# Seven-product second layer: the first product is copied by ScalarE into another product's PSUM bank, the products run in another order, and the sums of quarters come in fewer pieces

## Chip, cores and metric

The kernel runs on one core of one Trainium2 chip. The metric is the time of the program on the device, in microseconds (us), as the median of several runs. Beside the times there is one execution recorded by the hardware profiler; all durations of single instructions come from that one.

## What is computed

For 8 sequences of 576 tokens with 8 heads of width 64: attention over a sliding window of 128 keys with a bias that falls with the distance; then, for each token's 512 values, a normalisation, a layer of 512 to 2048 with a ReLU, a second layer of 2048 to 512, and the sum with the layer's input.

```python
scores = scale * q @ k.T - slope[head] * distance    # only 0 <= distance < 128, else -1e9
attn = softmax(scores)
x = concat_heads(attn @ v)                           # (8, 576, 512)
xn = (x - mean(x)) / sqrt(var(x) + 1e-6) * g_ln
out = x + maximum(xn @ w_ch1, 0.0) @ w_ch2           # (512 x 2048), (2048 x 512)
```

## The kernel before

**Blocks and groups.** The tokens are cut into 36 blocks of 128 (per pair of sequences 8 whole blocks and one, T, that holds the 64 last tokens of both). A block's attention gives a tile `x` of 128 tokens by 512. The two layers run on groups of blocks: groups 0 to 3 have two blocks each, groups 4 to 10 four. Group 10 has a form of its own for both layers (`mlp1_last`, `mlp2_last`). This text is about groups 4 to 9.

**First layer** (`mlp1`, matmuls in L866). Sixteen units, one for each 128 of the 2048 hidden values: four matmuls of 128x512 into one PSUM bank, then a ReLU to `ht_all`, by ScalarE (L882), or for units 6 and 13 by VectorE (L874).

**Second layer of groups 4 to 9** (`mlp2_seven`, matmuls in L1096). The 2x2 block product (512 tokens in a top and a low half, 2048 hidden values in two halves, 512 outputs in a left and a right half) is made with seven products in place of eight. Four of them take sums of quarters of the hidden values, made by VectorE in `sum_hidden` (L916): s1 = a21 + a22, s2 = s1 - a11, s3 = a11 - a21, s4 = a12 - s2. Each quarter is 128 x 8 x 256; a sum can be made in pieces of its 8 parts. A product is 16 matmuls of 128x256 into one PSUM bank (8 for each of the two blocks of a half, which lie side by side in the bank). It is cut into four units of four matmuls, so that the layer has units 0 to 27. Products add up in PSUM in three banks called x, t and y, and after each product VectorE adds the bank, scaled by the token's `rstd`, onto two output tiles `o` (`onto`, L1117, two instructions). The seven, in the order before:

| place | bank | product | then added onto |
|---|---|---|---|
| 1 | x (fresh) | a11 b11 | top left |
| 2 | t (fresh) | a12 b21 | top left |
| 3 | x | s2 t2 | top right |
| 4 | y (fresh) | s1 t1 | low right |
| 5 | x | s3 t3 | low right |
| 6 | y | s4 b22 | top right, then the top half is stored |
| 7 | x | a22 t4 | low left, then the low half is stored |

Because x goes on growing, product 3 may not start before `onto` has read what product 1 left in x, and product 5 not before `onto` has read what product 3 left.

**Order of the work.** The engines' orders are written out by hand: TensorE (PE) runs the units of the layers, and between them, at places listed in `TWICE` and `LEAD`, steps of the attention of later blocks. A block n has four steps: *go* (scores, and the exponential of one half of them, L509), *step* (values, L594, into PSUM; then on VectorE reciprocal L602, x L603, mean L631 and xc L635), *exps* (the exponential of the other half), and *rest* (VectorE multiplies the new probabilities by the mask, L531, one or two instructions; ScalarE squares xc, L679, for the variance; DMA transposes are issued). In groups 5 to 8 the first layer holds go, step, exps, rest of one block and go, step, exps of the next; the second layer holds *rest* and *go* behind unit 0, *step* and *exps* behind unit 5, *rest* behind 8, *go* behind 12, *step* and *exps* behind 19, *rest* behind 23. In group 9 only the first five of these nine are left. `weave_at` puts the pieces of sums of `SUMS_AT` behind a unit of the first layer, ahead of the attention steps of the same place; the dictionary `more` does the same with what it lists, for either layer (sums of first-layer weights for group 10, L916 too, and from unit 20 of group 9 on the sums of its inputs).

Each engine runs its instructions in the order in which they are written, and waits where a semaphore isn't there yet; what is written behind waits too.

Of the kernel before, what the change touches and what calls it, by code (L numbers as in the profile page):

```python
# [50 lines left out]
SUMS_AT = {  # L51
# [5 lines left out]
}  # L57


# [36 lines left out]
def kernel(  # L96
# [10 lines left out]
    nc = tc.nc  # L107
# [426 lines left out]
    def attends(p, blk):  # L534

        low, high, every = [0, 1], [2, 3], [0, 1, 2, 3]
        if blk == T:
            return [(p, T, [6, 7], m_ends, "probs", hps) for hps in (low, high)]
        if blk < 2:
            return [(p, blk, [blk], m_full[:, :, P:], "own", every)]  # L540
        return [(p, blk, [blk - 2, blk], m_full, "probs", hps) for hps in (low, high)]
# [5 lines left out]
    def tail_attend(p):  # L547
        return (p, T, [T], m_tail, "own", [0, 1, 2, 3])
# [169 lines left out]
    for g, size in enumerate(GROUPS):  # L718
        n = sum(GROUPS[:g])
# [67 lines left out]
    for n in range(8, ONE_GO):  # L787
        ahead = place[min(n + AHEAD, count - 1)]
        todo = []
# [23 lines left out]
    for n in range(ONE_GO, count):  # L813
        todo = []
        if n + 1 < count and order[n + 1][1] == T:
            todo.append(tail_attend(order[n][0]))
        if n + 2 < count:
            todo += attends(*order[n + 2])
        first_of, pairs = n == ONE_GO, (1, 0) if len(todo) > 1 else (0,)
        go = [(attend, *a, sc, first_of or sc == 1, sc == 0) for a, sc in zip(todo, pairs)]  # L820
        step = [(load_until, place[min(n + AHEAD, count - 1)]), (masks,) + order[n]]
        step += [(values_at_once, *order[n], 1), (centre,) + order[n]]
        rest = [(masks, *args[:2], 1) for args in todo] + [(square, n)]
        for tag, m in (("q", n + 5), ("k", n + 6)):
            if m < count and order[m][1] % 2 == 0:
                p, blk = order[m]
                (step if first_of else rest).append((turn_natural, tag, p, blk // 2))
        steps += [go, step, [(exps,)], rest]
    TWICE = [1, 4, 5, 7, 7, 11, 12], [0, 0, 5, 5, 8, 12, 19, 19, 23]
    LEAD = [([2, 2, 4, 4, 7, 7, 9, 9, 12, 13], TWICE[1])]  # L830
    LEAD += 4 * [TWICE] + [(TWICE[0], TWICE[1][:5]), ([], [])]
    done = 0

    def advance_to(n):
        nonlocal done
        while done < min(n, len(steps)):
            for f, *args in steps[done]:
                f(*args)
            done += 1
# [69 lines left out]
    half = NFB // 2  # L909
    left, right = slice(0, DM // 2), slice(DM // 2, DM)  # L910
    b11, b12 = w2[:, 0:half, left], w2[:, 0:half, right]
    b21, b22 = w2[:, half:NFB, left], w2[:, half:NFB, right]
    t1, t2, t3, t4 = (w2sums[:, i] for i in range(4))
# [148 lines left out]
    hsums = {}  # L1062
# [20 lines left out]
    def mlp2_seven(g):  # L1083


        ht = hidden[g]
        s = [hsums.pop((g, i)) for i in (1, 2, 3, 4)]
        a11, a12, a22 = ht[:, 0:half], ht[:, half:NFB], ht[:, half:NFB]

        def product(ps, lhs, off, rhs, first):  # L1090


            for pair in range(2):
                at = off + pair * P
                for fb in range(half):
                    nc.tensor.matmul(  # L1096
                        ps[:, pair, :],
                        lhs[:, fb, at : at + P],
                        rhs[:, fb, :],
                        start=(first and pair == 0 and fb == 0),  # L1100
                        stop=(fb == half - 1),
                        skip_group_check=True,
                    )
                    if fb % 4 == 3 and not (pair == 1 and fb == half - 1):
                        yield

        outs = {}

        def onto(ps, blocks, cols, fresh):

            for pair in range(2):
                at = 2 * blocks + pair
                p, blk = members[g][at]
                n = p * NSLOT + blk
                if at not in outs:
                    outs[at] = out_pool.tile([P, DM], FP32, tag="o", name="o")
                nc.vector.scalar_tensor_tensor(  # L1117
                    out=outs[at][:, cols],
                    in0=ps[:, pair],
                    scalar=rstd[:, n : n + 1],  # L1120
                    in1=(xs[p, blk] if fresh else outs[at])[:, cols],
                    op0=ALU.mult,
                    op1=ALU.add,
                )

        def leave(blocks, cols=slice(0, DM)):
            for pair in range(2):
                store(*members[g][2 * blocks + pair], outs[2 * blocks + pair], cols)

        def bank2():  # L1130
            t = ps_mm.tile([P, DM], FP32, tag="mm", name="ps_s")
            return t.rearrange("p (r d) -> p r d", r=2)

        top, low = 0, 1
        x = bank2()
        yield from product(x, a11, 0, b11, True)
        onto(x, top, left, True)
        yield
        t = bank2()
        yield from product(t, a12, 0, b21, True)  # L1140
        onto(t, top, left, False)
        yield
        yield from product(x, s[1], 0, t2, False)
        onto(x, top, right, True)
        yield
        y = bank2()
        yield from product(y, s[0], 0, t1, True)
        onto(y, low, right, True)
        yield
        yield from product(x, s[2], 0, t3, False)  # L1150
        onto(x, low, right, False)
        yield
        yield from product(y, s[3], 0, b22, False)
        onto(y, top, right, False)
        leave(top)
        yield
        yield from product(x, a22, 2 * P, t4, False)
        onto(x, low, left, True)
        leave(low)
        yield  # L1160
# [103 lines left out]
    def weave_at(units, *places, seven=None, sums=None, more={}):  # L1264


        advance_to(done + places.count(-1))
        for u, _ in enumerate(units):
            for f, *args in more.get(u, []):
                f(*args)  # L1270
            if seven is not None:
                if u == 1:
                    inv_std(sum(GROUPS[:seven]), len(members[seven]))
                for i, c in SUMS_AT.get(u, []):
                    sum_hidden(seven, i, c)
            if sums is not None and u % 4 == 1:
                sum_w2(sums + u // 4)
            advance_to(done + places.count(u))
# [13 lines left out]
    with tc.manual_schedule(engines={engine.PE}):  # L1292
        with tc.manual_schedule(engines={engine.Activation, engine.DVE, engine.SP, engine.Pool}):
            start()
            advance_to(first)
            weave_at(mlp1_pair((0, 12), (0, 8), (12, NFB), (8, NFB)), 1, 2, 3, 3, 7, 7, 9, 18, 24, 28)
            weave_at(mlp2(0, ((0, 8), (8, 12), (12, NFB))), 1, 4, 8, 10, 10, 12)
            weave_at(mlp2(1), 1, 3, 5, 7, 9, 13, 13)
            weave_at(mlp1(2), 0, 4, 7, 9, 14)
            weave_at(mlp2(2), 1, 5, 9, 13, 13, 15, 15)  # L1300

            weave_at(mlp1(3, (9, 10, 11)), 4, 7, 8, 10, 12, 15, sums=0)
            weave_at(mlp2(3), 0, 2, 3, 6, 9, 11, 12, sums=4)
            last = len(GROUPS) - 1
            for g in range(4, last):
                one, two = LEAD[g - 4]
                early, late = ({u: [(sum_w1, i)] for u, i in at.items()} for at in W1_SUMS_AT.get(g, ({}, {})))
                if g == last - 1:  # L1310
                    late[20] = [(sum_x, last, i) for i in (1, 2)]
                    late[24] = [(sum_x, last, i) for i in (3, 4)]
                    late[26] = [(inv_std, sum(GROUPS[:last]), len(members[last]))]
                weave_at(mlp1(g, (6, 13)), *one, seven=g, more=early)
                weave_at(mlp2_seven(g), *two, more=late)
            units = mlp2_last(last)
            scores_psum.close()
            ps_last = pool("ps_last", 1, space=PSUM)
            LAST_SUMS_AT = {
                u: [(sum_hidden, last, 3 + u % 2, (c, c + half // 2))]  # L1320
                for u, c in ((2, 0), (4, half // 2), (3, 0), (5, half // 2))
            }
            mlp1_last(last, lambda: next(units), ps_last)
            weave_at(units, more=LAST_SUMS_AT)
# [31 lines left out]
```

## Time and profile before

| | us |
|---|---|
| median of 3 runs | 309.24 (308.67 to 309.47) |
| the profiled execution | 309.44 |
| its span, first to last instruction | 307.7 |
| granted TensorE clock over the span | 0.994 |
| TensorE matmuls busy | 294.9 (96%) |
| VectorE busy | 240.7 (78%) |
| ScalarE busy | 180.1 (59%) |
| groups 4 to 9, both layers | about 94 to 279 us of the span |
| group 10 and the last stores | about 279 to 307.7 us |

A line of the timeline reads: start in us from the span's beginning, duration of the (merged) instructions in us, engine, line, operation, output <- inputs with shapes, xcount, and in brackets how long the engine had been idle before and what released it. DVE is VectorE, ACT is ScalarE, PEld TensorE's weight loads. A 128x256 matmul is recorded with 0.27 us, but the next one starts 0.109 us later: eight of them are in the records as 1.03 or 1.04 us and keep TensorE for 0.87. So the idle time that the profile gives for TensorE behind a matmul is about 0.16 us less than the time by which the next matmul was late, and in this text a delay of TensorE is counted from start to start.

### The profile page before, as it was taken

Reading aid. Unit: us, or ns where it says so; the run is one execution under the profiler, and the core shown is the slowest. Engines: PE = TensorE matmul, PEld = TensorE weight load, DVE = VectorE, ACT = ScalarE, POOL = GpSimd, SP = SyncE. Lnnn points to the kernel's source line nnn. Section 1 sums busy time; section 2 is a strip of 40 time slices with the busy share of each in tenths; the row PEclk is TensorE's granted clock in tenths of the full one; section 3 lists DMA queues with packets and bytes.
Section 4 is the critical chain, followed back from the end, with each engine's and each line's share of the span. In section 5 each row is a group of like instructions: output and inputs, shape, how many; then the busy total and the mean of one; then the engine's idle time right before and its main releaser. Section 6 shows DMA issues by size and latency. Waiting matters only on the chain.

```text
span 307.7 us, 9278 instructions
## 1 busy us (share of the span) xinstructions
PE 294.9 (96%) x3778; PEld 201.8 (66%) x3778; DVE 240.7 (78%) x646; ACT 180.1 (59%) x332; POOL 112.5 (37%) x153
## 2 busy tenths in 40 slices
PE   6799999999999999999999999999999999899994
PEld 2377745866855568656765686468656865688883
DVE  2578868779896698759876987598889878968993
ACT  4487776858967863477347734773577357405500
POOL 8933559783773480684017161760000000000000
PEclk9799999999999999999999999999999999999999
DMA  9999999999999999999979999999472053005014
GB/s 96 171 200 201 191 152 154 200 141 100 142 127 160 163 143 144 166 183 150 120 120 130 148 116 152 141 132 133 89 129 46 19 87 86 19 19 137 2 34 102
DMA packets 150074, 38.03 MB, mean 124 GB/s; under 512 B 140656, under 2 KB 145920, under 8 KB 150032
## 3 DMA queue, kind: packets, MB, share of 16 engines
q0 software_dynamic: 103792, 18.46, 86.9%
q1 hardware_dynamic: 45760, 18.60, 39.8%
q8 instruction: 29, 0.48, 0.7%
q10 hardware_dynamic: 480, 0.39, 0.5%
q14 instruction: 13, 0.11, 0.1%
HBM read 36.90 MB, written 9.44 MB: 151 GB/s over the span
## 4 chain that ended last, share of the span: by engine, by line
PE 75%; DVE 13%; DMA 5%; ACT 2%; issue 2%; POOL 1%; DVEq 0%; POOLq 0%
PE ps_m L866 28%; PE ps_s L1096 18%; PE ps_m L896 9%; PE ps_sc L498 5%; DVE s L916 5%; PE ps_q L1175 4%; PE ps_sc L594 4%; DMA xT<-xc 3%; PE ps_x L990 3%; DVE probs L531 2%; DVE x L603 2%; DMA first<-in_k_dram 2%; DVE o L1117 1%; DVE xc L635 1%; PE ps_tr L346 1%
## 5 line engine op out<-in xcount | busy, mean ns | idle before, releaser
L866 PE MATMUL ps_m<-xT,w1g 128*128 128x512 f16 (+1 forms) x512 | 104.0, 353 | 0.1
L882 ACT ACTIVATE ht_all<-ps_m 128x512 f16<-128x512 f32 (+1 forms) x143 | 71.3, 512 | 35.2 <-PE ps_m L866 32.7
L866 PEld LDWEIGHTS <-w1g 128*128 128x128 f16 x512 | 47.7, 98 | 41.4 <-issue 0.3
L509 ACT ACTIVATE probs<-ps_sc 128x1024 f16<-128x1024 f32 x56 | 55.6, 1021 | 8.9 <-PE ps_sc L498 8.7
L289 POOL DMA_DIRECT2D vx<-in_v_dram x40 | 34.1, 862 | 72.4 <-PE ps_sc L594 59.4
L1096 PE MATMUL ps_s<-w,s 128*128 128x256 f16 x384 | 44.9, 273 | 2.0 <-DVE o L1117 2.0
L1096 PEld LDWEIGHTS <-s 128*128 128x128 f16 x384 | 36.8, 98 | 7.4 <-issue 2.8
L679 ACT ACTIVATE junk<-xc 128x512 f16<-128x512 f16 x28 | 17.6, 629 | 40.3 <-DVE xc L635 40.3
L531 DVE TENSOR_TENSOR probs<-probs,m 128x1024 f16<-128x1024 f16 x56 | 36.2, 683 | 2.0 <-ACT probs L509 2.0
L1096 PE MATMUL ps_s<-w,ht_all 128*128 128x256 f16 x288 | 35.2, 273 | 0.0
L896 PE MATMUL ps_m<-w,ht_all 128*128 128x512 f16 x128 | 31.5, 380 | 0.0
L1096 PEld LDWEIGHTS <-ht_all 128*128 128x128 f16 x288 | 27.4, 98 | 4.6
L278 POOL DMA_DIRECT2D q<-in_q_dram x40 | 27.6, 708 | 4.1 <-PE ps_m L866 1.9
L916 DVE TENSOR_TENSOR s<-ht_all 128x1024 f16<-128x1024 f16 (+2 forms) x36 | 20.5, 568 | 7.9 <-ACT ht_all L882 7.0
L498 PEld LDWEIGHTS <-k 64*64 64x64 f16 x1088 | 16.1, 108 | 13.7 <-issue 12.5
L498 PE MATMUL ps_sc<-q,k 64*64 64x128 f16 (+1 forms) x1088 | 22.1, 215 | 1.0 <-issue 0.7
L603 DVE SCALAR_TENSOR_TENSOR x<-ps_sc,rec 128x512 f16<-128x512 f32 x32 | 22.1, 691 | 1.1
L1117 DVE SCALAR_TENSOR_TENSOR o<-ps_s,rstd,x 128x256 f32<-128x256 f32 x48 | 20.8, 475 | 2.2 <-PE ps_s L1096 2.2
L275 POOL DMA_DIRECT2D k<-in_k_dram x20 | 17.9, 911 | 6.8 <-DMA k<-k 5.6
L1117 DVE SCALAR_TENSOR_TENSOR o<-ps_s,rstd,o 128x256 f32<-128x256 f32 x36 | 15.7, 477 | 5.8 <-PE ps_s L1096 5.7
L602 DVE RECIPROCAL rec<-ps_sc 128x8 f32<-128x8 f32 x32 | 6.4, 201 | 16.8 <-PE ps_sc L594 16.7
L594 PEld LDWEIGHTS <-probs 128*128 128x128 f16 x384 | 15.9, 98 | 3.6
(117 smaller groups left out, 376.6 us busy)
## 6 DMA issues: line engine op xcount, KB each, us to landing
out_dram<-o SPq DMA_DIRECT2D x64, 128.0 KB, 3.4
vx<-in_v_dram POOLq DMA_DIRECT2D x32, 128.0 KB, 7.5
w<-in_moe_w_ch_dram POOLq DMA_DIRECT2D x8, 512.0 KB, 11.7
k<-in_k_dram POOLq DMA_DIRECT2D x30, 128.0 KB, 7.5
q<-in_q_dram POOLq DMA_DIRECT2D x48, 64.0 KB, 6.2
q<-in_q_dram POOLq DMA_DIRECT2D x10, 128.0 KB, 7.3
out_dram<-o SPq DMA_DIRECT2D x10, 64.0 KB, 1.9
k<-in_k_dram POOLq DMA_DIRECT2D x8, 64.0 KB, 7.2
```

The source lines that it names most:

```text
L289: nc.gpsimd.dma_start(out=vx[p0 : p0 + n, :, 0:D], in_=v[b, :, t0 : t0 + n, :].rearrange("h p d -> p h d"),)
L498: nc.tensor.matmul(in_halves(ps[cols, j, n, t, :])[:, r, queries], kt[rows, hp, cols], in_halves(qt[rows, b, hp])[:, r, queries], start=no ...
L509: nc.scalar.activation(out=dst.rearrange("p (n j) q -> p j n q", j=2), in_=ps.rearrange("p j n t q -> p j n (t q)"), func=AF.Exp, scale=in ...
L531: nc.vector.tensor_tensor(out=dst, in0=dst, in1=mask, op=ALU.mult)
L594: nc.tensor.matmul(ps[:, h, 0 : D + 1], pr[:, h, t, :], vext[(p * NSLOT + o) % NV][:, h, :], start=(n == 0), stop=(n == len(terms) - 1),)
L603: nc.vector.scalar_tensor_tensor(out=x.rearrange("p (h d) -> p h d", h=H), in0=ps[:, :, 0:D], scalar=1.0, in1=rec.unsqueeze(2).broadcast_t ...
L866: nc.tensor.matmul(ps[:, 0:cols], w[:, kb, fb * P : (fb + 1) * P], xT[:, kb, 0:cols], start=(kb == 0), stop=(kb == NKB - 1),)
L882: nc.scalar.activation(out=ht[:, fb, :], in_=ps[:, 0:cols], func=AF.Relu)
L896: nc.tensor.matmul(sums[at], ht[:, fb, at * P : (at + 1) * P], w2[:, fb, :], start=(fb == 0), stop=(fb == NFB - 1),)
L916: nc.vector.tensor_tensor(out=out, in0=a, in1=b, op=op)
L1096: nc.tensor.matmul(ps[:, pair, :], lhs[:, fb, at : at + P], rhs[:, fb, :], start=(first and pair == 0 and fb == 0), stop=(fb == half - 1), ...
L1117: nc.vector.scalar_tensor_tensor(out=outs[at][:, cols], in0=ps[:, pair], scalar=rstd[:, n : n + 1], in1=(xs[p, blk] if fresh else outs[at] ...
```

## The change

In `mlp2_seven` all three banks are taken at the start. After product 1 VectorE no longer adds x onto the output; ScalarE copies bank x into bank t (128x512, fp32), and the product a12 b21 is later accumulated in t on top of the copy, so that one `onto` adds both. The places are now: 1 x: a11 b11, copy to t; 2 y: s1 t1, onto low right; 3 x: s2 t2, onto top right; 4 t: a12 b21, onto top left; 5, 6 and 7 as before. So a group has six `onto` in place of seven.

The sums of quarters: before, s1, s2 and s4 came in three pieces each (parts 0 to 2 behind unit 11 of the first layer, 3 to 5 behind unit 14, 6 and 7 behind unit 15). Now s1 has the same three pieces, s2 two (parts 0 to 2 behind unit 11, 3 to 7 behind unit 15), and s4 is one instruction over all 8 parts, behind unit 4 of the second layer. s3 stays.

In the attention of blocks 12 to 35, the squaring of a block with n % 4 = 1 moves from its own *rest* to the *rest* of block n + 2. In group 9 the *rest* of block 34 moves from behind unit 0 of the second layer to behind unit 14 of the first, after the piece of s1 there.

```diff
 SUMS_AT = {
     5: [(3, (0, 4))],
     8: [(3, (4, 8))],
-    11: [(1, (0, 3)), (2, (0, 3)), (4, (0, 3))],
-    14: [(1, (3, 6)), (2, (3, 6)), (4, (3, 6))],
-    15: [(1, (6, 8)), (2, (6, 8)), (4, (6, 8))],
+    11: [(1, (0, 3)), (2, (0, 3))],
+    14: [(1, (3, 6))],
+    15: [(1, (6, 8)), (2, (3, 8))],
 }
...
-        rest = [(masks, *args[:2], 1) for args in todo] + [(square, n)]
+        rest = [(masks, *args[:2], 1) for args in todo]
+        rest += [(square, m) for m in {1: (), 3: (n - 2, n)}.get(n % 4, (n,))]
...
-    LEAD += 4 * [TWICE] + [(TWICE[0], TWICE[1][:5]), ([], [])]
+    LEAD += 4 * [TWICE] + [(TWICE[0] + [14], TWICE[1][1:5]), ([], [])]
...
-        s = [hsums.pop((g, i)) for i in (1, 2, 3, 4)]
+        s = [hsums[g, i] for i in (1, 2, 3)]
...
         top, low = 0, 1
-        x = bank2()
+        x, t, y = bank2(), bank2(), bank2()
         yield from product(x, a11, 0, b11, True)
-        onto(x, top, left, True)
+        nc.scalar.copy(out=t, in_=x)
         yield
-        t = bank2()
-        yield from product(t, a12, 0, b21, True)
-        onto(t, top, left, False)
+        yield from product(y, s[0], 0, t1, True)
+        onto(y, low, right, True)
         yield
         yield from product(x, s[1], 0, t2, False)
         onto(x, top, right, True)
         yield
-        y = bank2()
-        yield from product(y, s[0], 0, t1, True)
-        onto(y, low, right, True)
+        yield from product(t, a12, 0, b21, False)
+        onto(t, top, left, True)
         yield
         yield from product(x, s[2], 0, t3, False)
         onto(x, low, right, False)
         yield
-        yield from product(y, s[3], 0, b22, False)
+        yield from product(y, hsums[g, 4], 0, b22, False)
         onto(y, top, right, False)
...
+                late[4] = [(sum_hidden, g, 4, (0, half))]
                 weave_at(mlp1(g, (6, 13)), *one, seven=g, more=early)
                 weave_at(mlp2_seven(g), *two, more=late)
```

The order in which SyncE and GpSimd issue their transfers is the same in both kernels, and so are the numbers of matmuls.

## The prediction, made before the changed kernel was run

> **What bounds the kernel now.** I read the page first (busy shares), then TensorE's waits, then the timeline around each change from first to second layer, since only groups 4 to 9 are touched.
>
> ```profile
> PE 294.9 (96%) x3778; PEld 201.8 (66%) x3778; DVE 240.7 (78%) x646; ACT 180.1 (59%) x332; POOL 112.5 (37%) x153
> ```
> ```profile
> PE ps_s L1096 <- DVE o L1117: 2.0, 5, 0.7
> ...
> PE ps_sc L594 <- DVE own L531: 0.8, 1, 0.8
> ```
>
> TensorE is the bound, and no matmul is added or removed, so the change can only win time in which TensorE waits. Both lines lie in these groups: five waits for `onto`, and one for a mask. Group 5 shows how the first kind arises:
>
> ```profile
> 141.89 0.60 ACT L882 ACTIVATE ht_all<-ps_m 128x512 f16<-128x512 f32 x1 [0.27 <-PE ps_m L866]
> 141.91 0.56 DVE L916 TENSOR_TENSOR s<-ht_all 128x768 f16<-128x768 f16 x1
> ...
> 143.10 0.56 DVE L916 TENSOR_TENSOR s<-ht_all,s 128x768 f16<-128x768 f16 x1
> 143.58 0.42 DVE L916 TENSOR_TENSOR s<-ht_all 128x512 f16<-128x512 f16 x1
> ...
> 144.49 0.43 DVE L916 TENSOR_TENSOR s<-ht_all,s 128x512 f16<-128x512 f16 x1
> 144.83 1.29 DVE L531 TENSOR_TENSOR probs<-probs,m 128x1024 f16<-128x1024 f16 x2
> 145.20 1.03 PE L1096 MATMUL ps_s<-w,ht_all 128*128 128x256 f16 x8
> 146.03 0.87 DVE L1117 SCALAR_TENSOR_TENSOR o<-ps_s,rstd,x 128x256 f32<-128x256 f32 x2
> 146.82 0.20 DVE L602 RECIPROCAL rec<-ps_sc 128x8 f32<-128x8 f32 x1
> 146.96 2.34 PE L1096 MATMUL ps_s<-w,s 128*128 128x256 f16 x20 [0.72 <-DVE o L1117]
> ```
> ```profile
> 148.42 0.63 ACT L679 ACTIVATE junk<-xc 128x512 f16<-128x512 f16 x1 [3.50 <-DVE xc L635]
> ...
> 150.23 0.87 DVE L1117 SCALAR_TENSOR_TENSOR o<-ps_s,rstd,x 128x256 f32<-128x256 f32 x2
> ```
>
> VectorE is busy without a gap from 141.14 to 151.1: six pieces of sums, two masks, and only then the `onto` that product 3 needs. The eight matmuls that began at 145.20 hold TensorE until 146.07; product 3 starts at 146.96, so it is 0.89 late (0.72 in the record, which counts the pipelined end). ScalarE stands idle for 3.50 us at that time.
>
> Start to start, the delays are: group 4, product 3 0.90; group 5, 0.89 and at product 5 0.08; group 6, 0.33 and 0.34; group 7 none; group 8, 0.33 and 0.08; group 9, 1.02 at the values (a next matmul at 268.45 after one at 267.40). Sum 3.97 us: the most that can be won here. In the last 28 us, which the change doesn't touch, TensorE loses 0.15 in one place.
>
> **The change, part by part.**
>
> *Product 3's wait* goes from VectorE to ScalarE. The copy has a row of its own form in group 10:
>
> ```profile
> L1007 ACT COPY ps_t<-ps_x 128x512 f32<-128x512 f32 x4 | 2.4, 597 | 7.7 <-PE ps_x L990 7.7
> ```
>
> In group 5 product 1 ends at 144.06 (12 matmuls from 142.75); with the 0.27 that ScalarE's rows show behind a matmul the copy runs from 144.33 to 144.93. Product 2 now stands between: product 3 would start at 146.07 without a delay, 1.1 later. Behind the copy in ScalarE's queue stands the exponential of the other half, 0.9 later than before (to 145.9); its mask is due at about 148, and its PSUM half is wanted by the scores of 149. The six copies of 0.6 so lie in this idle time (3.50 here, 2.32 at the least, in group 7) and cost nothing; if that cover were gone, each would cost up to 0.6.
>
> *Product 2 is now s1 t1.* It needs the last piece of s1 two products (32 matmuls) earlier than before. That piece waits for unit 15's ReLU (until 142.49) and one piece takes 0.42: done at 142.95. Weights of parts 6 and 7 are the seventh load of product 2, due at 144.06 + 0.66 = 144.7. Margin 1.8 us. The other groups have the same order; in group 9 a mask (0.60) and a square (0.81 on ScalarE, ahead of unit 15's ReLU) come in between, and about 0.8 is left.
>
> *VectorE's chain* decides what product 5 finds. From unit 15's ReLU on, the order is s1 (6,8), s2 (3,8), two masks, s4, then the same reciprocal, x, xc, `onto`, masks, `onto` as before. Pieces of 512, 768 and 1024 elements take 424, 558 and 683 ns: 0.506 ns an element, so 1280 are estimated at 0.81 and 2048 at 1.20 us. A piece that needs the one before starts 0.04 behind its end (141.91 to 142.51), one that doesn't starts 0.08 ahead of it (143.10 to 143.58; two masks step by 0.60). So: 0.03 + 0.46 + 0.73 + 1.20 + 1.12 = 3.54 from the ReLU's end to the reciprocal, and in group 5 that is 146.03 in place of 146.82. The two removed `onto` instructions (0.80) are the whole gain: the sums behind the ReLU weigh the same (142.51 to 144.83 before, 2.32; now 0.46 + 0.73 + 1.12), since all of s4 now stands there, and the piece that unit 11 no longer has (0.59) only makes VectorE wait for that ReLU. From the reciprocal to the end of the second `onto` the old timeline takes 4.28 (146.82 to 151.10), and nothing in it changes.
>
> The unknown is the two long sums, which no row shows. From below, they cost no less than one row of 1024 each (0.68 each, 0.65 less in all, and the gain is the full 3.97); from above, one element a cycle as the fp32 row of the same line suggests (693 ns for 512). I take the line through the f16 rows, whose layout is the same.
>
> With this, product 5 starts at the later of its own undelayed time and the end of `onto` + 0.05:
>
> | group | product 5 before | without delays | `onto` ready | gain |
> |---|---|---|---|---|
> | 4 | 120.04 | 119.14 | 119.10 | 0.90 |
> | 5 | 151.15 | 150.18 | 150.36 | 0.79 |
> | 6 | 182.26 | 181.59 | 181.80 | 0.46 |
> | 7 | 212.63 | 212.63 | 212.21 | 0 |
> | 8 | 243.30 | 242.89 | 242.84 | 0.41 |
>
> (ReLU ends: 111.23, 142.49, 173.72, 204.94, 234.98; group 6 takes 4.49 behind the reciprocal, group 7 has one mask.)
>
> *Group 9's rest* moves behind unit 14: the mask (267.71 before, for which the values wait until 268.45) is then done by 265.3. Gain 1.02. Product 5 there has 0.7 of margin.
>
> *The squares* move to where ScalarE idles: one fewer (0.62 + 0.19) in the first layer, where four waits of VectorE for a ReLU sum to 7.0 us, one more ahead of the square at 148.42, inside the 3.50. No engine on the path gets shorter, so I count nothing. xc has five buffers and is held two blocks longer. `inv_std` reads them a layer later.
>
> Products 6 and 7 and the next group's banks: s4 is done 6 us ahead of product 6; `onto` of t comes where that of y came; unit 0 and 1 of the next group take banks free since then. Nothing new is late there. Transfers keep order, and follow TensorE as before (GpSimd waits 59.4 us in all for the values' matmuls before it may load).
>
> Sum: 0.90 + 0.79 + 0.46 + 0.41 + 1.02 = 3.58. Against the profiled execution, 309.44 - 3.58 = **305.9 us** (its span 307.7 becomes 304.1, and 1.74 lie around it). The median of the runs shown is 309.24, so that is a median about 3.4 below.
>
> One rule of the Trainium skill speaks against part of this. Its page "VectorE: DVE Perf Modes", section "The DRAIN you can't avoid", says that behind every VectorE instruction the pipeline empties before the next starts. The trace doesn't agree for instructions without a wait between them (two masks of 0.68 in 1.29), and the same page allows an earlier start in its section on two instructions with no wait. Priced by the drain, the four early starts in my chain fall away, which is the first rival below.
>
> **Rivals.**
>
> 1. *The delay moves to product 5.* If VectorE's chain is 0.32 longer (no early start of 0.08 at four places), `onto` is ready at 119.42, 150.68, 182.12 and 243.16: gains 0.62, 0.47, 0.14, 0.14 and 1.02, in all 2.4: 307.0. If it isn't shorter than before at all, only group 9 gains: 308.4. For it: groups 5 and 6 already end on the `onto` column. Against: 0.80 of work leaves the chain, and the early starts are in the rows.
>
> 2. *Slower.* The long sums run at half speed. Then s2 and s4 take 0.506 x (1280 + 2048) = 1.68 more ahead of the reciprocal, and product 5 is late against its undelayed time by 1.64, 1.86, 1.89, 1.26, 1.63 and in group 9 by 0.93: 9.2 lost, 3.97 won, **314.7**. It decides from 0.8 more per group on, where the late products add up to 3.97. For it: no f16 row of the line is longer than 1024. Against: three lengths on one straight line, with the same runs of 256.
>
> 3. *Loads become the bound* in groups 4 to 6: the page's DMA row stands at 9 up to 215 us. Then 2.15 of the gain is lost: 308.0. Against: no wait of TensorE for a transfer appears in these groups.
>
> That the change doesn't do what it says I rule out for time: the banks and the order are as written in the built program, and an overwrite in t would take as long as an addition.
>
> **How the numbers follow.** Forecast (305.3 to 306.6): 0.64. Rival 1: 0.20 (306.6 to 308.6), of which 0.06 ends within 0.3%. Rival 2 and other ways to be slower: 0.08. Rival 3: 0.05. More than 3.97 won: 0.03. Runs of this kernel differ by about 0.3% (0.9 us), so that less than that can't be told from no change. Faster: 0.64 + 0.14 + 0.05 + 0.03 = 0.86; same 0.06; slower 0.08. The range takes the forecast, the drain case and rival 3: 305.2 to 308.1, which leaves out 0.17.
>
> **What the new profile should show.** TensorE's wait for `onto` falls from 2.0 to under 0.4 in its record, and what remains is at product 5 of groups 5 and 6; the wait for `own` is gone; no wait of TensorE for ScalarE's copy or for s1 appears; L1117 has 72 instructions in place of 84; one 128x2048 row of about 1.20 us; from ReLU 15 to the reciprocal 3.54. I am wrong if the copy starts late behind an exponential, if s1's last piece holds product 2, or if the 2048 row is near 2 us.

## The result, and the profile after

The changed kernel takes 305.21 us (median of 6 runs, 304.51 to 307.49) against 309.31 (6 runs, 308.67 to 311.02): ratio 0.9877, interval 0.9832 to 0.9922 (the record's estimate over all runs; the quotient of the two medians is 0.9867). Its profiled execution took 304.59 us with a span of 302.8.

The page of the changed kernel, first part (busy us, share of the span, instructions), and the first line of its chain of waits:

```profile
PE 294.7 (97%) x3778; PEld 201.8 (67%) x3778; DVE 232.3 (77%) x616; ACT 184.4 (61%) x338; POOL 113.8 (38%) x153
...
PE 88%; DMA 5%; DVE 3%; ACT 1%; issue 1%; POOL 1%; DVEq 0%; ACTq 0%; POOLq 0%
```

TensorE does the same work. VectorE has 8.4 us and 30 instructions less, ScalarE 4.3 us and 6 instructions more. In the chain VectorE's share was 13% before and is 3% now: the waits for `onto` linked TensorE's chain to VectorE's.

All waits of TensorE in the changed kernel (us in total, times, longest):

```profile
PE ps_warm L334 <- DVE vx L1290: 1.5, 1, 1.5
PE ps_tr L414 <- DMA first<-in_k_dram: 0.9, 2, 0.6
PE ps_tx L655 <- DVE xc L635: 0.5, 1, 0.5
PE ps_sc L498 <- DVE k L420: 0.4, 1, 0.4
PE ps_sc L498 <- ACT q L439: 0.3, 1, 0.3
PE ps_sc L498 <- DMA q<-q: 0.2, 1, 0.2
```

Neither the row for `onto` nor that for `own` is left, and none for ScalarE's copy or for a sum has come. (Two lines were added above L1096, so that the second layer is L1098 now, `onto` L1119, the sums L918 and the copy L1140.)

Group 5 in the timeline of the changed kernel, the place that was shown of before:

```profile
139.81 0.60 ACT L884 ACTIVATE ht_all<-ps_m 128x512 f16<-128x512 f32 x1 [0.27 <-PE ps_m L868]
...
140.44 0.43 DVE L918 TENSOR_TENSOR s<-ht_all 128x512 f16<-128x512 f16 x1 [0.73 <-ACT ht_all L884]
...
140.90 0.83 DVE L918 TENSOR_TENSOR s<-s,ht_all 128x1280 f16<-128x1280 f16 x1
...
141.64 1.29 DVE L531 TENSOR_TENSOR probs<-probs,m 128x1024 f16<-128x1024 f16 x2
...
141.98 1.04 PE L1098 MATMUL ps_s<-w,s 128*128 128x256 f16 x8
142.23 0.57 ACT L1140 COPY ps_s<-ps_s 128x512 f32<-128x512 f32 x1 [0.30 <-ACT probs L509]
...
142.84 1.22 DVE L918 TENSOR_TENSOR s<-ht_all,s 128x2048 f16<-128x2048 f16 x1
...
143.12 2.78 PE L1098 MATMUL ps_s<-w,s 128*128 128x256 f16 x24
...
143.98 0.20 DVE L602 RECIPROCAL rec<-ps_sc 128x8 f32<-128x8 f32 x1
...
147.40 1.79 DVE L1119 SCALAR_TENSOR_TENSOR o<-ps_s,rstd,x 128x256 f32<-128x256 f32 x4
...
148.32 0.92 PE L1098 MATMUL ps_s<-w,s 128*128 128x256 f16 x7
```

The copy runs behind product 1 while TensorE runs product 2, and TensorE goes on without a delay: the 24 matmuls from 143.12 are the second half of product 2 and all of product 3. From the end of unit 15's ReLU (140.41) to the reciprocal VectorE takes 3.57. What is left late is product 5: the `onto` of product 3 is the first pair of the four from 147.40, and TensorE starts 0.22 late at 148.32.

**One measure for all kernels.** The start of group 4's second layer lies between 108.69 and 112.40 us in the twelve profiles of this study, in no order that fits the kernels; 1.38 of the 4.85 by which the profiled time fell was there already (110.43 before, 109.05 after). So below I use M, the time from the first second-layer matmul of group 4 to the last of group 9, and add up what was late in it, start to start. Before: M 168.20 with 3.97 late; so nothing late would be 164.23. After: 164.71. By groups, 4 to 9, product starts won 0.93, 0.75, 0.63, 0, 0.39 and 1.02; 0.23 is lost again by a wait of the first unit of group 5's first layer for the transposed xc.

That wait, called W, appears in four of the twelve profiles (0.23 after, 0.40 in E4, 1.42 in E1, and with slower matmuls behind it 3.97 in E3) and is taken out of M where said. The profile of E3 was taken at a granted clock of 0.988 over the span and its time is the longest of that kernel's runs, so only the delays at its product 5 are read.

| kernel | median | ratio to before, interval | M | late in M (us) |
|---|---|---|---|---|
| before | 309.1 to 309.3 | | 168.20 | product 3 or 5: 2.95; values of group 9: 1.02 |
| changed | 305.21 | 0.9877 (0.9832 to 0.9922) | 164.71 | W 0.23; product 5: 0.22 |
| E1 order and copy only | 307.28 | 0.9925 (0.9898 to 0.9953) | 167.37 | W 1.42; product 5: 0.70; values: 1.02 |
| E2 sums only | 309.44 | 1.0007 (0.9979 to 1.0036) | 168.03 | product 5: 3.71; values: 0.10 |
| E3 copy on VectorE | 307.63 | 0.9943 (0.9917 to 0.9969) | 171.02 | W and slower matmuls: 3.97; product 5: 2.84 |
| E4 rest back | 306.08 | 0.9888 (0.9855 to 0.992) | 164.96 | W 0.40; product 5: 0.21; values: 0.10 |
| E5 s4 behind unit 12 | 304.68 | 0.9863 (0.983 to 0.9896) | 164.23 | nothing |
| E6 squares back | 305.40 | 0.9888 (0.9849 to 0.9928) | 164.47 | product 5: 0.21 |
| E7 rest only | 307.84 | 0.9968 (0.9949 to 0.9988) | 167.35 | product 3 or 5: 2.86; product 3 of group 9: 0.25 |
| E8 s4 twice | 311.65 | 1.0072 (1.0046 to 1.0098) | 170.58 | product 5: 6.37 |
| E9 old sums | 305.23 | 0.9875 (0.9839 to 0.9911) | 164.71 | product 5: 0.09; product 2 of group 9: 0.39 |
| E10 copy in the old order | 310.48 | 1.0051 (1.0025 to 1.0078) | 169.40 | product 2: 5.19 |

In every row the delays and 164.23 give M within 0.04.

### The profile page after: what moved, and what is told of

It reads as the page before. It is cut to its first block, busy times and chain, and to the rows that moved or that the text cites. A ratio compares the mean times of both kernels' runs of the same rounds, so it can differ in the third digit from the quotient of the medians.

```text
span 302.8 us, 9262 instructions
## 1 busy us (share of the span) xinstructions
PE 294.7 (97%) x3778; PEld 201.8 (67%) x3778; DVE 232.3 (77%) x616; ACT 184.4 (61%) x338; POOL 113.8 (38%) x153
## 4 chain that ended last, share of the span: by engine, by line
PE 88%; DMA 5%; DVE 3%; ACT 1%; issue 1%; POOL 1%; DVEq 0%; ACTq 0%; POOLq 0%
PE ps_m L868 35%; PE ps_s L1098 22%; PE ps_m L898 9%; PE ps_sc L498 5%; PE ps_sc L594 5%; PE ps_q L1176 4%; PE ps_x L992 3%; DMA q<-q 3%; DMA first<-in_k_dram 2%; PE ps_warm L334 1%; PE ps_tr L346 1%; DVE probs L531 1%; POOL first L190 1%; PE ps_pv L565 1%; PE ps_tx L655 1%
## 5 line engine op out<-in xcount | busy, mean ns | idle before, releaser
L289 POOL DMA_DIRECT2D vx<-in_v_dram x40 | 35.3, 893 | 65.1 <-PE ps_sc L594 47.2
L1098 PE MATMUL ps_s<-w,s 128*128 128x256 f16 x384 | 45.7, 273 | 0.1
L1098 PEld LDWEIGHTS <-s 128*128 128x128 f16 x384 | 36.8, 98 | 4.4 <-issue 0.2
L531 DVE TENSOR_TENSOR probs<-probs,m 128x1024 f16<-128x1024 f16 x56 | 36.3, 685 | 1.8 <-ACT probs L509 1.8
L1098 PE MATMUL ps_s<-w,ht_all 128*128 128x256 f16 x288 | 36.1, 273 | 0.0
L1098 PEld LDWEIGHTS <-ht_all 128*128 128x128 f16 x288 | 27.3, 98 | 5.0
L918 DVE TENSOR_TENSOR s<-ht_all 128x1024 f16<-128x1024 f16 (+2 forms) x36 | 20.5, 570 | 11.6 <-ACT ht_all L884 10.6
L1119 DVE SCALAR_TENSOR_TENSOR o<-ps_s,rstd,x 128x256 f32<-128x256 f32 x48 | 20.9, 477 | 2.6 <-PE ps_s L1098 2.2
L898 PEld LDWEIGHTS <-ht_all 128*128 128x128 f16 x128 | 11.0, 98 | 10.6
```

The source lines that it names most:

```text
L289: nc.gpsimd.dma_start(out=vx[p0 : p0 + n, :, 0:D], in_=v[b, :, t0 : t0 + n, :].rearrange("h p d -> p h d"),)
L531: nc.vector.tensor_tensor(out=dst, in0=dst, in1=mask, op=ALU.mult)
L898: nc.tensor.matmul(sums[at], ht[:, fb, at * P : (at + 1) * P], w2[:, fb, :], start=(fb == 0), stop=(fb == NFB - 1),)
L1098: nc.tensor.matmul(ps[:, pair, :], lhs[:, fb, at : at + P], rhs[:, fb, :], start=(first and pair == 0 and fb == 0), stop=(fb == half - 1), ...
L1119: nc.vector.scalar_tensor_tensor(out=outs[at][:, cols], in0=ps[:, pair], scalar=rstd[:, n : n + 1], in1=(xs[p, blk] if fresh else outs[at] ...
```

## The experiments

The theory: the gain of groups 4 to 8 comes from taking one `onto`, two instructions of 0.80 together, out of VectorE's chain, which the copy on ScalarE and the new order make possible. The rivals: it comes from the shorter sums, or from group 9's moved *rest*, or the order alone would do.

**E1: the new order and the copy alone** (sums, squares and *rest* as before; written here against the changed kernel).

```diff
-    11: [(1, (0, 3)), (2, (0, 3))],
-    14: [(1, (3, 6))],
-    15: [(1, (6, 8)), (2, (3, 8))],
+    11: [(1, (0, 3)), (2, (0, 3)), (4, (0, 3))],
+    14: [(1, (3, 6)), (2, (3, 6)), (4, (3, 6))],
+    15: [(1, (6, 8)), (2, (6, 8)), (4, (6, 8))],
...
-        rest = [(masks, *args[:2], 1) for args in todo]
-        rest += [(square, m) for m in {1: (), 3: (n - 2, n)}.get(n % 4, (n,))]
+        rest = [(masks, *args[:2], 1) for args in todo] + [(square, n)]
...
-    LEAD += 4 * [TWICE] + [(TWICE[0] + [14], TWICE[1][1:5]), ([], [])]
+    LEAD += 4 * [TWICE] + [(TWICE[0], TWICE[1][:5]), ([], [])]
...
-                late[4] = [(sum_hidden, g, 4, (0, half))]
```

> The second layer as changed (ScalarE's copy, new order of products), but sums of quarters in the old nine pieces, squares and group 9's rest where they were. The measure is the stretch from the first second-layer matmul of group 4 to the last of group 9: 168.20 us before, 164.71 with the whole change. Theory (VectorE's work from unit 15's ReLU to the second onto decides; the change takes two instructions, 0.80, out of it and the sums weigh the same there): the gains of groups 4 to 8 stay, 2.5, group 9's 1.0 is missing: 165.7, time about 306.7. Rival (the fewer pieces of sums are what shortens VectorE's chain): product 5 is late instead, under 1 us is won: 167.3 or more, time 308.4 or more.

Measured: 307.28, M 165.95 without W. The time is 0.6 above the theory's 306.7; the rival's 308.4 lies outside its interval (306.1 to 307.8, as 0.9898 to 0.9953 of 309.25). From TensorE's waits in it (us in total, times, longest):

```profile
PE ps_m L866 <- DMA xT<-xc: 1.3, 1, 1.3
...
PE ps_sc L594 <- DVE own L531: 0.8, 1, 0.8
...
PE ps_s L1096 <- DVE o L1117: 0.4, 1, 0.4
```

Of the five waits for `onto` one is left in the records, at product 5. Order and copy alone win 2.25. Of the 0.70 left at product 5, 0.55 is in group 5, where the centring took 0.83 in place of 0.35 (the last section looks at such rows).

**E2: the sums alone** (kernel before, with the new pieces, s4 behind unit 4 of the second layer).

```diff
-    11: [(1, (0, 3)), (2, (0, 3)), (4, (0, 3))],
-    14: [(1, (3, 6)), (2, (3, 6)), (4, (3, 6))],
-    15: [(1, (6, 8)), (2, (6, 8)), (4, (6, 8))],
+    11: [(1, (0, 3)), (2, (0, 3))],
+    14: [(1, (3, 6))],
+    15: [(1, (6, 8)), (2, (3, 8))],
...
-        yield from product(y, s[3], 0, b22, False)
+        yield from product(y, hsums[g, 4], 0, b22, False)
...
+                late[4] = [(sum_hidden, g, 4, (0, half))]
```

> The kernel before with nothing but the sums in five pieces (s4 in one, behind unit 4 of the second layer). Theory: product 3 starts in time, since s4 no longer stands ahead of the onto that it needs, but product 5 finds VectorE where it was, so groups 4 to 8 gain nothing and the delay only moves; in group 9 the mask stands behind less and comes at 267.4 in place of 268.4, 0.95 won: stretch 167.2, time 308.3. Rival (fewer pieces are the gain): 2.5 or more won, stretch 165.7 or less.

Measured: 309.44, M 168.03. The theory expected 167.2 and 308.3, and missed: group 9's part came (0.92 won), but groups 4 to 8, which it had at no change, lost 0.76. Group 5 in the timeline of E2:

```profile
145.99 0.87 DVE L1117 SCALAR_TENSOR_TENSOR o<-ps_s,rstd,x 128x256 f32<-128x256 f32 x2
...
146.78 1.22 DVE L916 TENSOR_TENSOR s<-ht_all,s 128x2048 f16<-128x2048 f16 x1
...
147.13 2.35 PE L1096 MATMUL ps_s<-w,s 128*128 128x256 f16 x20
147.91 0.20 DVE L602 RECIPROCAL rec<-ps_sc 128x8 f32<-128x8 f32 x1
...
152.25 0.92 PE L1096 MATMUL ps_s<-w,s 128*128 128x256 f16 x7 [0.83 <-DVE o L1117]
```

Product 3 is on time, since `onto` now stands ahead of s4; but s4 then delays the `onto` for product 5, which is 0.99 late (0.97 in two places before). In groups 4 to 8 product 5 is late by 0.76, 0.99, 0.81, 0.39 and 0.76, in all 3.71 where it was 2.95. Fewer pieces do not make the chain shorter (from unit 15's ReLU to the reciprocal it takes 4.36 in group 5, 4.33 before); in groups 6 to 8 they make it start later. Before, VectorE worked from unit 14 on without a wait; with fewer pieces it waits up to 0.97 for unit 15's ReLU. What it gains by having less to do early, it can't use. That was not in the theory's 167.2.

**E3: the copy on VectorE.**

```diff
-        nc.scalar.copy(out=t, in_=x)
+        nc.vector.tensor_copy(out=t, in_=x)
```

> The whole change, but VectorE makes the copy from x to t. Theory: VectorE's chain is longer by one instruction of about 0.69, 0.61 start to start; product 5 is late by 0.58, 0.62, 0.58, 0.2, 0.57 and 0 more in groups 4 to 9: stretch 167.2, time 307.7. Rival (the new order, with a whole product between the two uses of x, is enough whoever reads x): stretch 164.7, time 305.2.

Measured: 307.63. One row of its groups and one of its waits:

```profile
L1140 DVE COPY ps_s<-ps_s 128x512 f32<-128x512 f32 x6 | 4.2, 692 | 0.0
```
```profile
PE ps_s L1098 <- DVE o L1119: 2.0, 4, 0.6
```

The same order with one instruction of 0.69 back in VectorE's chain: product 5 is late by 0.58, 0.81, 0.67, 0.20 and 0.58, in all 2.84, and M without W is 167.05. So the new order with its one `onto` less is not enough while VectorE makes the copy; the work has to leave VectorE.

**E4: group 9's *rest* put back**, all else as changed.

```diff
-    LEAD += 4 * [TWICE] + [(TWICE[0] + [14], TWICE[1][1:5]), ([], [])]
+    LEAD += 4 * [TWICE] + [(TWICE[0], TWICE[1][:5]), ([], [])]
```

> The whole change, but group 9's rest step stays behind unit 0 of the second layer. The prediction gave that move the whole 1.02 of group 9. Theory now: with s2 and s4 later, the mask there is done at about 267.45 of the old timeline where the values are due at 267.43, so the move itself is worth 0.1 and no more: stretch 164.8. Rival (as predicted): 1.0 lost, stretch 165.7, time 306.2.

Measured: 306.08, M 164.56 without W. Its time alone would not decide, since the rival said 306.2 and the interval (0.9855 to 0.992) overlaps that of the changed kernel; the timeline does. At group 9's values, first before and then in E4:

```profile
267.71 0.68 DVE L531 TENSOR_TENSOR own<-own,m_tail 128x1024 f16<-128x1024 f16 x1
...
268.45 0.20 PE L594 MATMUL ps_sc<-vx,own 128*128 128x65 f16 x1 [0.85 <-DVE own L531]
```
```profile
262.73 0.69 DVE L531 TENSOR_TENSOR own<-own,m_tail 128x1024 f16<-128x1024 f16 x1
...
263.31 0.23 PE L594 MATMUL ps_sc<-vx,probs 128*128 128x65 f16 x2
...
263.47 0.20 PE L594 MATMUL ps_sc<-vx,own 128*128 128x65 f16 x1
```

The values are 0.10 late, not 1.02. With the shorter list of sums ahead of it the mask starts 0.58 before the values at its old place; before, it started 0.34 after them (267.71 and 267.37).

**E7: group 9's *rest* alone**, in the kernel before (E4's edit the other way round).

> The kernel before with nothing but group 9's rest step moved behind unit 14. Theory: 1.02 won in group 9, nothing elsewhere: stretch 167.2, time 308.3. If e4 shows the move to be worth 0.1 in the whole change, the two gains are two ways to the same 1.0 and don't add up. Rival (the mask ahead of the last pieces of sums delays product 3 of group 9 by the same time): nothing won, 168.2.

Measured: 307.84, M 167.35, where the theory had 167.2: 0.85 of M is won, 0.77 of it in group 9. There the values are on time, but product 3 is 0.25 late in their place, a part of what the rival expected. With E4: either the moved *rest* or the shorter sums is enough for most of group 9's 1.02.

**E5: s4 later**, behind unit 12 of the second layer in place of unit 4. Only product 6 needs it.

```diff
-                late[4] = [(sum_hidden, g, 4, (0, half))]
+                late[12] = [(sum_hidden, g, 4, (0, half))]
```

> The whole change, with s4 behind unit 12 of the second layer in place of unit 4, so behind the second onto in VectorE's queue. Theory: what is left of the delays goes: 0.2 at product 5 of group 5, and 0.2 at the start of group 5's first layer, which waits for a transposed xc that is now issued 1.1 earlier: stretch 164.3, a time of 304.8, under what the times can tell. Rival (product 6 then waits for s4): a wait of up to 1 us at product 6 in each group, stretch above 166.

Measured: 304.68, M 164.23. In group 5 of its timeline:

```profile
147.00 0.87 DVE L1119 SCALAR_TENSOR_TENSOR o<-ps_s,rstd,x 128x256 f32<-128x256 f32 x2
147.79 1.22 DVE L918 TENSOR_TENSOR s<-ht_all,s 128x2048 f16<-128x2048 f16 x1
...
148.30 1.91 PE L1098 MATMUL ps_s<-w,s 128*128 128x256 f16 x16
```

`onto` is ahead of s4, and product 5 starts on time. No second-layer matmul of groups 4 to 9 is late any more: 168.20 - 164.23 = 3.97, all that could be won. Its time and the changed kernel's can't be told apart.

**E6: the squares back** in their own *rest*.

```diff
-        rest = [(masks, *args[:2], 1) for args in todo]
-        rest += [(square, m) for m in {1: (), 3: (n - 2, n)}.get(n % 4, (n,))]
+        rest = [(masks, *args[:2], 1) for args in todo] + [(square, n)]
```

> The whole change, but each block is squared in its own rest step. Theory: ScalarE's queue is off the path in both places: stretch 164.7 within 0.1, time 305.2. Rival (the ReLUs of units 8 to 10, later by 0.8 behind that square, hold s1's first piece and with it VectorE's chain): 0.3 or more a group, stretch 166 or more.

Measured: 305.40, M 164.47, as changed without W (164.48). Moving the squares is worth nothing that shows here.

**E8: s4 made twice** (the same instruction again, for its time).

```diff
-                late[4] = [(sum_hidden, g, 4, (0, half))]
+                late[4] = 2 * [(sum_hidden, g, 4, (0, half))]
```

> The whole change, with s4 computed twice in a row, which adds 1.14 to 1.22 to VectorE's chain and nothing else. Theory: product 5 is late by about 1.1, 1.15, 1.1, 0.7, 1.1 and 0.4 more in groups 4 to 9: stretch 170.2, time 310.7, slower than the kernel before. Rival (VectorE has room here, 77% busy): stretch 164.7 to 165.5.

Measured: 311.65, M 170.58. The row of its waits:

```profile
PE ps_s L1098 <- DVE o L1119: 5.4, 5, 1.3
```

1.22 more in the chain makes product 5 late by 1.24, 1.48, 1.35, 0.87, 1.24 and 0.19. It is the prediction's second rival made real, with 1.22 a group in place of 1.68. Take 0.42 from each and 4.08 is left: so 0.8 more a group is, by this estimate, where the change would stop paying, as the prediction had it.

**E9: the old pieces of the sums**, all else as changed (E2's edit the other way round).

> The changed kernel with the old pieces of the sums (s4 again in three pieces, s2 in three); copy, new order, squares and the place of the rest stay. Measure: start of the first second-layer matmul of group 4 to that of the last one of group 9, without waits for a transfer at the start of a first layer; 168.20 before, 164.23 if nothing is late. Theory (the copy and the order free VectorE's chain of two instructions, and how the sums are cut is worth next to nothing): only product 5 is late, 0.15 in group 4 and about 0.1 in group 5 (up to 0.55 if that run's centring happens to be stretched beside a GpSimd issue), none in group 9, since the mask lies behind unit 14: 164.4 to 164.9, time 305.2 to 305.8. Rival (the shorter list of pieces is part of the gain): the 0.70 at product 5 that the order alone left stays and the mask of group 9 is late again by 0.93: 165.9 and 306.9.

Measured: 305.23, M 164.71. The changed kernel has the same M with W's 0.23 in it; E9 has no W, and 0.48 late in place of 0.22. In groups 4 to 8 it is only 0.09. The rest sits elsewhere than expected, in group 9 at product 2:

```profile
264.01 0.69 DVE L531 TENSOR_TENSOR own<-own,m_tail 128x1024 f16<-128x1024 f16 x1
...
264.62 0.42 DVE L918 TENSOR_TENSOR s<-ht_all 128x512 f16<-128x512 f16 x1
...
265.09 0.39 PE L1098 MATMUL ps_s<-w,s 128*128 128x256 f16 x2 [0.22 <-DVE s L918]
```

Behind three old pieces and the moved mask the last piece of s1 comes at 265.04, and product 2's seventh matmul waits 0.39 for it. In the changed kernel it is ready at 262.40 and wanted at about 263.3 (262.65 + 6 x 0.109).

**E10: the copy in the old order** (products 2 and 4 exchanged).

```diff
         nc.scalar.copy(out=t, in_=x)
         yield
-        yield from product(y, s[0], 0, t1, True)
-        onto(y, low, right, True)
+        yield from product(t, a12, 0, b21, False)
+        onto(t, top, left, True)
...
-        yield from product(t, a12, 0, b21, False)
-        onto(t, top, left, True)
+        yield from product(y, s[0], 0, t1, True)
+        onto(y, low, right, True)
```

> The changed kernel with products 2 and 4 exchanged, so that the product which adds onto the copied bank follows straight behind the first, as in the order before; all else as changed. Theory (the new order is what hides the copy): each of the six second products waits for the first product's end, 0.27 of release and a copy of 0.57, so it starts 0.85 to 0.90 late, six times 5.1 to 5.4; the 0.2 at product 5 of group 5 is absorbed. Same measure: 169.3 to 169.6, time 310.2 to 310.6. Rival (other matmuls and loaded weights between the two products cover the copy, so the order does not matter): under 0.2 a group, 164.5 to 165.4 and 305.3 to 306.4.

Measured: 310.48, M 169.40. The row of its waits:

```profile
PE ps_s L1098 <- ACT ps_s L1140: 4.2, 6, 0.7
```

Each group's second product is 0.865 late: 0.27 for the release, 0.57 for the copy, and the issue behind it. The new order is what hides the copy; without it the kernel is slower than before, by 0.5% (0.25 to 0.78).

## Why the prediction was right, step by step

**The sum.** 3.58 was predicted; M without W fell by 3.72, with W by 3.49. Group 4 gives 0.03 more than its term because the prediction's table has 120.04 for the start of product 5 there, which is the end of `onto`; product 5 started at 120.09 and was 0.03 late already.

| group | 4 | 5 | 6 | 7 | 8 | 9 |
|---|---|---|---|---|---|---|
| predicted | 0.90 | 0.79 | 0.46 | 0 | 0.41 | 1.02 |
| measured | 0.93 | 0.75 | 0.63 | 0 | 0.39 | 1.02 |

**Product 3's wait and the copy**: as predicted. The copy took 0.570 in place of 0.6. In group 5 it started about 0.26 behind the end of product 1 (the exponential ahead of it in ScalarE's queue had ended 0.30 before) and ended at 142.80, 2.9 us before product 4. E10 gives the price without the cover: 0.865 a group.

**VectorE's chain**: as predicted, 3.57 against 3.54. The two long sums took 0.825 and 1.220 against 0.81 and 1.20. The spacing of its steps in the timeline (a step starts 0.03 behind the end of the one before, or 0.08 to 0.09 ahead of it) is that of the short rows. By the Trainium skill's page "VectorE: DVE Perf Modes", section "The DRAIN you can't avoid", under which the next instruction starts only when the pipeline is empty, the chain would have been an estimated 3.86 (3.54 and four times the 0.08 of an early start); the trace of the changed kernel does not agree with that for these instructions. It fits the exception that the same section makes, an earlier start for a next instruction that is not held.

**"The two removed `onto` instructions (0.80) are the whole gain"**: right for groups 4 to 8. E3 puts 0.69 back and loses 2.6 of M; E9 undoes the sums, and in groups 4 to 8 less is late than in the changed kernel (0.09 against 0.22). The claim beside it, that the sums behind the ReLU weigh the same, holds for group 5 (0.99 late in E2, 0.97 before) and within 0.14 for group 4; in 6 to 8 the new pieces alone cost 0.14, 0.39 and 0.35 in E2, since VectorE was ahead of the ReLU there before.

**Group 6** was mis-sized: 0.46 predicted, 0.63 measured. I took 4.49 from the reciprocal to the end of the second `onto` there, from the profile of before, as a property of the group; it was 4.29 after (174.46 to 178.75). The difference is one centring instruction: 0.57 in the one execution, 0.35 in the other. The longer row stood beside an issue of GpSimd (last section); it is 0.56 in E7 and 0.35 in E2, so it was no property of the group.

**Group 9's *rest***: the number was right, and its cause was credited to the wrong step. The prediction gave the whole 1.02 to the moved *rest*; E4 shows that with the new sums only 0.10 hangs on it. The two edits are each a cover for the other: without both 1.02 is late (E1), without the move 0.10 (E4), without the new sums 0.39 (E9), at another product. The prediction's price for the sums was zero, which with the new order is about right in groups 4 to 8 (E9), but not in group 9. That its 1.02 came out is luck in so far as either edit would have given most of it.

**s1's margin** of 1.8 in group 5 is 1.8 (140.87 against 142.6), and about 0.9 in group 9 (0.8 predicted).

**The rivals.** Of the first, 0.22 at product 5 of group 5 remains (0.18 was in the forecast's table); the 0.21 that the table left in group 6 did not come. The second has its price in E8. The third came in small, 0.23 at group 5's first layer: the transposed xc was issued at 114.96 and took 8.6 us to land (117.29 and 7.2 before). Why it varies so is open; it is as large as 1.42 in E1 with the old sums, and absent from E5, E6, E9 and E10. It was not tried by itself.

**The time.** 305.9 was forecast from the profiled execution and a median about 3.4 below: 305.8. It is 305.21, just under the 305.3 at which the forecast's own part of the range began, and 0.01 inside the whole range. The median fell by 4.10, more than the 3.97 that could be won in groups 4 to 9, while M fell by 3.49. No run shows where the other 0.6 comes from; the six runs lie 3 us apart, so that it may be chance. What the runs bear out is the account of the delays, and that the time still fell inside the range is in part luck. Nor do the profiled executions show a larger gain: of their 4.85, 1.38 lies ahead of group 4.

## What to carry to other kernels

When one engine waits for another, ask what stands ahead of the awaited instruction in its queue, and move work off that queue; here 0.8 us less on VectorE in a group is worth 2.3 to 2.7 over five groups, and cutting the same sums in other pieces nothing there (in the old order, E2, it even lost 0.76). A copy on an idle engine was free here only with independent work of the waiting engine behind its producer (E10): the order had to be changed with it. And issue what is needed late, late: s4 behind unit 12 removes the last delay of these groups, and no other delay comes for it.

## What was not expected of the hardware

The centring L635 (f16, 512 elements, one tensor and a scalar for each partition) has two prices. In the profiles of eleven of the kernels (all but E3) 164 such rows have no transfer issue of GpSimd beside them, and all take 0.352 to 0.357 us. Of 232 that do, 150 take no more than that either, and 82 up to 0.83. In group 5 of E1, GpSimd and VectorE:

```profile
148.34 1.79 POOL L275 DMA_DIRECT2D k<-in_k_dram  x2
...
148.53 0.83 DVE L635 TENSOR_SCALAR xc<-x,mean 128x512 f16<-128x512 f16 x1
```

The long ones begin about 0.2 to 0.6 us behind the start of an issue. For issues of 0.69 to 0.70 us, rows that began 0.19, 0.24, 0.27 and 0.37 into one took 0.62, 0.57, 0.54 and 0.45: all end 0.81 or 0.82 behind its start, as if the instruction waited for something that GpSimd holds in the later part of an issue. The masks (L531), which read two f16 tensors, have a median of 0.684 beside issues (87 rows) and without (111) in the changed kernel, E5 and E6.

The Trainium skill's page "SBUF — State Buffer", section "SBUF: two separate sides", says that VectorE and GpSimd share one pair of memory ports, that some forms of VectorE instruction need it, and that whichever starts first keeps it for its whole instruction while the other is blocked. The rows agree that VectorE is held up; but 132 of the 150 short rows began inside an issue and were not held up, which speaks against the pair being held through a whole issue. That the ports are the cause is not shown by any run here.

It cost 0.48 at product 5 in E1, and made group 6's term wrong in the prediction.
